# Set places for the softmax exponentials and the first unit rows, squares shared between two engines, and earlier scores of the third batch

## The chip, the core and the metric

One core of a Trainium2 chip runs the whole program. The metric is the device time of one execution in microseconds, so smaller is better; the median of several runs is what kernels are compared by. The engines are TensorE (PE in the profile, its weight loads PEld), VectorE (DVE), ScalarE (ACT), GpSimd (POOL) and SyncE (SP). The last two issue most of the DMA transfers here. Each engine works through its own list of instructions in order, and an instruction whose operands are not ready holds up all that stand behind it in that list.

## What is computed

A channel attention over q, k and v for four batches, and a feed-forward block on its output:

```python
B, N, C = (4, 6080, 256)            # d_ff = 2048
qn = q / (np.linalg.norm(q, axis=1, keepdims=True) + 1e-06)
kn = k / (np.linalg.norm(k, axis=1, keepdims=True) + 1e-06)
s = kn.transpose(0, 2, 1) @ qn / tau
s = s - s.max(-1, keepdims=True)
a = np.exp(s)
a /= a.sum(-1, keepdims=True) + 1e-09
x = (v @ a).reshape(B * N, C)
h = x @ w_in
out = np.maximum(0.01 * h, h) @ w_out
```

The scores s are only 256x256 for each batch, but they sum over all 6080 rows. Since a is small, the kernel multiplies it into w_in once for each batch (w), and the feed-forward block then reads v directly.

## The kernel before

**The feed-forward block.** A batch's 6080 tokens are cut into six tiles of up to 512, 24 tiles in all. A tile is worked off in eight *periods* (d_ff in eight pairs of 128), 192 in all, each about 10 to 12 us long; a period's number is tile times eight plus pair. Each period forms its block of h from seven products of blocks (a Strassen-like scheme; L1197, into the PSUM banks x and z, three passes each over the high and low parts of weights and v) and multiplies the activated blocks by w_out (L1628, into the banks o). ScalarE copies h out of PSUM (L1254), applies the activation (g, L1211) and makes its high part (g_split, L1211 and L1218); VectorE adds to h from PSUM (L1248) and makes the low part (L1222). There is one bank x and one bank z: the next product into them has to wait until ScalarE has read the last one. At a period's end ScalarE copies bank x into bank z (L1243), the *seed copy*, on which the next period's product into z is built up. The last cast of g in a period belongs to the block called C21. From period 48 the feed-forward block works in 16-bit floats, before that in 32-bit ones.

**The attention between it.** While a batch's tiles are worked off, the attention of the next one is woven in by a planner. Steps are put into queues (act, act_late, dve, dve_idle, pe, pe_next) with an estimated length; at fixed places of each period a slot with some room takes the steps that fit, in order, if a step's condition (ready) holds. The number spots[0] counts the visits of TensorE's own queue, three a period. All this happens when the program is written: what stands in the program is a fixed list for each engine.

A batch's scores take 48 chunks of 128 rows, two to a group. For the second and third batch each chunk is cast (L375, ScalarE), its low part is taken (L379, VectorE), its square is added up (L313, L316) and TensorE multiplies it (L408); SCORES_AT gives the period in which this begins. Then follow the norms, the scaled scores (L615), the row maxima nm (L624, VectorE), two exponentials (L630, ScalarE), the turned blocks (L668 and L697 on ScalarE, L676 and L704 on VectorE), and the new weights, whose high and low parts (w_first, w_rest; L866, L878) are stored to DRAM on SyncE's queue (L901) or GpSimd's (L921) and loaded again period by period.

The fourth batch (UNIT) does it another way: ahead of its scores all of q and k is loaded once (L294, GpSimd's queue, three buffers in the tile spare), squared in place by ScalarE (square_ahead, L322) and added up by an accumulating DMA (L327, L325; GpSimd's queue), whose end frees the buffer for the load three groups on. Later the rows are loaded a second time, scaled to unit length (L360, VectorE), cast (unit_high, L366, ScalarE), split (L370, VectorE) and multiplied (L408). The casts write halves of the tile qk_split, of which three exist; the same three hold w_first and w_rest until their stores have read them. The class Splits keeps account of which halves are open.

```python
SCORES_AT = {1: (8, 12), 2: (40, 16), 3: (0, 0)}
...
at(now[0] + 1, put, "act_late", 0.6, lambda j=j: sc.square_ahead(j), then)
...
], ready=splits.free)
```

Of the kernel before, what the change touches and what calls it, by code (L numbers as in the profile page):

```python
# [14 lines left out]
AF = mybir.ActivationFunctionType  # L15
ALU = mybir.AluOpType
AX = mybir.AxisListType

P = 128
QUAD = 32  # L20
TW = 512
G = 2
# [10 lines left out]
TOP = 12  # L33
SUMS_AT = (73, 77, 80, 105)
UNITS = 5
SCORES_AT = {1: (8, 12), 2: (40, 16), 3: (0, 0)}
AHEAD_AT = 49
G_SCALE = 2.0**-19
G_LESS = 2.0**-2
# [4 lines left out]
def channel_attention_ffn(  # L44
# [17 lines left out]
    nc = tc.nc  # L62
    B, N, C = q.shape
    CH = C // P
# [5 lines left out]
    REST = N - RPP * P  # L70
    NCHUNK = RPP + (1 if REST else 0)
# [11 lines left out]
    LEAN = 2  # L83
# [11 lines left out]
    def bank(tag, bufs=1):  # L95
        return psum.tile([P, TW], F32, name="ps_" + tag, tag=tag, bufs=bufs)

    def temp(dtype=F32, name="temp"):
        return work.tile([P, TW], dtype, name=name, tag="temp", bufs=TEMPS)
# [28 lines left out]
    def spare_part(n0, n1):  # L128
        if spare[0] is None:
            spare[0] = const.tile([P, NF * C], F32, name="spare", tag="spare")  # L130
        return spare[0][:, n0 * TW:n1 * TW]
# [26 lines left out]
    class Scale:  # L158
# [3 lines left out]
        def __init__(self, name, parts, bufs=1, near=False):  # L162
            t = small.tile([P, 16], F32, name=name, bufs=bufs)
            self.most = t[:, 0:parts]
            self.top, self.e, self.up, self.down, self.out, self.minus = (t[:, x:x + 1] for x in range(8, 14))
            self.near = near
            if not near:
                self.line = dram.tile([P, 1], F32, name=name + "_line", bufs=bufs)
            self.seen = 0
# [56 lines left out]
    class Splits:  # L226


        def __init__(self):
            self.open, self.half = [], None  # L230

        def free(self, whole=False):
            return self.half is not None and not whole or sum(1 for n in self.open[-3:] if n) < 3 and not (
# [20 lines left out]

        def close(self, n):
            self.open[n] -= 1

    splits = Splits()

# [3 lines left out]
    class Scores:  # L263
# [51 lines left out]
        def add_square(self, sq):  # L315
            return nc.vector.tensor_tensor(out=self.acc[0], in0=self.acc[0], in1=sq, op=ALU.add)  # L316

        def square_ahead(self, j):

            n = REST if REST and j == NCHUNK - 1 else P  # L320
            own = self.chunk(j)[0:n]
            ins = nc.scalar.activation(out=own, in_=own, func=AF.Square)  # L322
            i, x = self.of[j]
            if REST and i == len(self.groups) - 1:
                nc.gpsimd.dma_start(out=self.totals[0:n, :, x, :], in_=own, accum_op=ALU.add)  # L325
            elif x == G - 1:
                nc.gpsimd.dma_start(  # L327
                    out=self.totals.rearrange("p x g c -> p (x g c)"),
                    in_=self.raw[i].rearrange("p x g c -> p (x g c)"), accum_op=ALU.add if i else ALU.bypass,
                )  # L330
            return ins

        def totals_added(self):
            self.total = self.totals[:, :, 0, :]
# [286 lines left out]

        def maxima(self):
            self.nm = small.tile([P, CH], F32, name="nm")
            return nc.vector.tensor_reduce(out=self.nm, in_=self.e, axis=AX.X, op=ALU.max, negate=True)  # L624

        def exps(self):
# [212 lines left out]
    now, w_done, w_stores = [0], {}, []  # L839
# [824 lines left out]
    def at(w, fn, *args):  # L1664
        steps.setdefault(w, []).append((fn, args))

    spots = [0]
# [31 lines left out]
    def put(queue, length, fn, then=(), first=False, ready=lambda: True):  # L1699


        def run():
            ins = fn()
            for entry in then:
                if entry[0] == "call":
                    entry[1](*entry[2:])
                else:
                    put(*entry)
            return ins

        run.ready = ready
        (todo[queue].appendleft if first else todo[queue].append)((length, run))
# [64 lines left out]
    def ahead_work(sc, i):  # L1777

        if i == 0:
            sc.totals = spare_part(6, 8).rearrange("p (x g c) -> p x g c", x=2, g=G)  # L1780
        raw = spare_part(i % 3 * 2, i % 3 * 2 + 2).rearrange("p (x g c) -> p x g c", x=2, g=G)
        sc.load(i, raw, (nc.gpsimd, nc.gpsimd))
        for j in sc.groups[i]:
            then = []
            if j == NCHUNK - 1:
                then = [("call", lambda: at(now[0] + 2, unit_norms, sc))]
            elif j == sc.groups[i][-1] and i + 3 < len(sc.groups):
                then = [("call", ahead_work, sc, i + 3)]
            at(now[0] + 1, put, "act_late", 0.6, lambda j=j: sc.square_ahead(j), then)

    def unit_norms(sc):
        put_steps([
# [6 lines left out]
    def load_next(sc):  # L1799
        if sc.loaded < len(sc.groups):  # L1800
            issued["load"] = sc.load(sc.loaded, qk_raw())
            sc.loaded += 1
# [5 lines left out]
    def unit_go(sc):  # L1808
        while unit_waits and len(unit_ahead) < UNITS and len(unit_temps) < 3:
            unit_one(sc, unit_waits.popleft())  # L1810

    def unit_one(sc, j):
        unit_ahead.append(j)
        unit_temps.append(j)
        t = []

        def unit():
            t.append(temp(name="unit").rearrange("p (x c) -> p x c", x=2))
            ins = sc.unit(j, t[0])
            if j % G == G - 1:  # L1820
                load_next(sc)
            return ins

        def product():
            unit_ahead.pop(0)
            unit_go(sc)
            splits.close(sc.at[j])
            if j == 0:
                sc.begin(None, bank("s"))
            mm = sc.product(j)  # L1830
            if j == NCHUNK - 1:
                norm_work(sc)
            return mm

        def low():
            unit_temps.remove(j)
            unit_go(sc)
            return sc.unit_low(j, t[0])

        def high():  # L1840
            put("act", 0.6, lambda: sc.unit_high(j, t[0]), [
                ("dve", 0.7, low, [("call", lambda: put(
                    "pe_next", 1, product, ready=lambda: (sc.b - 1, "products") in w_done
                ))])
            ], ready=splits.free)

        put("dve", 0.7, unit, [("call", high)])

    def norm_work(sc):
# [18 lines left out]
                ("dve", 0.7, sc.inverse, lambda: not reading[0])]  # L1868

    def softmax(sc):  # L1870
        return [*[("act", 0.65, sc.exps)] * CH,
                ("dve", 1.1, sc.normed), ("call", turn_work, sc)]

    def turn_work(sc):
# [385 lines left out]
    for b in range(1, B):  # L2260
        w0 = (b - 1) * WPB
        sc = scores[b]
        begin, span = SCORES_AT[b]
        when = {j: begin + j * span // NCHUNK for j in range(NCHUNK)}
# [30 lines left out]
    sc, nxt = scores[0], scores[1]  # L2295
# [185 lines left out]
    for i in range(NTILES):  # L2481
        for p in range(NPAIR):
# [15 lines left out]
            x, y, z = bank("x"), bank("z" if i else "y"), None if seeded else bank("z")  # L2498
# [121 lines left out]
```

## Time and profile before

| | us |
|---|---|
| median of three runs | 2030.99 |
| lowest and highest run | 2030.10, 2033.97 |
| the profiled execution | 2031.82 |
| its span, first to last instruction | 2030.04 |
| TensorE busy | 2019.1 |
| VectorE busy | 1684.6 |
| ScalarE busy | 1573.9 |
| GpSimd busy | 394.7 |

The span is the profile's, the median that of the timed runs; the rows further down come from the profiled execution. Times in a timeline count from the span's start. A bracket behind a row gives the time for which that engine was idle before it and the instruction that ended the idle time; a row without one started behind its predecessor.

### The profile page before, as it was taken

The page shows a single profiled execution, that of the slowest core. Times are in us where ns is not written, and L with a number is a line of the kernel's source. Part 1 is how long each engine was busy: PE and PEld are TensorE (multiplying, and loading weights), DVE is VectorE, ACT ScalarE, POOL GpSimd, SP SyncE. Part 2 cuts the span into 40 slices and gives each one's busy share as a digit, 9 for nine tenths or more (in the row PEclk, how much of TensorE's full clock was granted, in tenths as well). Part 3 has the DMA queues.
Part 4 walks back from the last instruction along what each step waited for, and adds up shares of the span by engine and source line. Part 5 has one row for each costly group of instructions (what it writes and reads, how often), then busy time and mean ns, then how long its engine had stood idle before and what let it go on. Part 6 is the DMA issues. An engine that isn't in the chain of part 4 may idle for free.

```text
span 2030.0 us, 28026 instructions
## 1 busy us (share of the span) xinstructions
PE 2019.1 (99%) x9474; PEld 1178.7 (58%) x9474; DVE 1684.6 (83%) x3153; ACT 1573.9 (78%) x2914; POOL 394.7 (19%) x495
## 2 busy tenths in 40 slices
PE   9999999999999999999999999999999999999999
PEld 8888888888885554444555444444444444444444
DVE  7988897787777788779888688989889988988976
ACT  6567886665778888777776678988988888898886
POOL 0000000001002222301000013434333433433342
PEclk9999999999999999999999999999999999999999
DMA  9946784667556977733232325767778876777774
GB/s 361 409 159 225 248 276 150 216 228 202 183 161 223 268 194 201 171 110 108 95 109 93 105 87 120 151 141 145 145 143 192 167 154 135 151 146 145 137 136 95
DMA packets 155727, 349.52 MB, mean 172 GB/s; under 512 B 17824, under 2 KB 49056, under 8 KB 155584
## 3 DMA queue, kind: packets, MB, share of 16 engines
q0 software_dynamic: 62752, 129.07, 32.1%
q1 hardware_dynamic: 92608, 218.48, 31.5%
q8 instruction: 74, 1.21, 0.3%
q14 instruction: 69, 0.57, 0.1%
q10 hardware_dynamic: 224, 0.20, 0.0%
HBM read 188.61 MB, written 57.42 MB: 121 GB/s over the span
## 4 chain that ended last, share of the span: by engine, by line
PE 96%; DVE 2%; ACT 1%; issue 0%; DMA 0%; DVEq 0%; ACTq 0%
PE ps_o L1628 25%; PE ps_x L1197 24%; PE ps_z L1197 18%; PE ps_o L1354 13%; PE ps_s L408 4%; PE ps_y L1354 3%; PE ps_s L1354 3%; PE ps_o L408 2%; PE ps_s L1995 1%; PE ps_y L408 1%; PE ps_y L1995 0%; DVE g_split L1222 0%; DVE h L1248 0%; PE ps_y L825 0%; PE ps_o L1377 0%; PE ps_y L1197 0%
## 5 line engine op out<-in xcount | busy, mean ns | idle before, releaser
L1197 PE MATMUL ps_x<-v_split,w_split 128*128 128x512 f16 (+3 forms) x2280 | 619.6, 380 | 2.6 <-ACT h L1254 2.5
L1628 PE MATMUL ps_o<-g_split,w_out_split 128*128 128x512 f16 (+3 forms) x2496 | 616.1, 382 | 0.0
L1197 PEld LDWEIGHTS <-w_split 128*128 128x128 f16 x3024 | 292.6, 98 | 347.7 <-issue 11.4
L1197 PE MATMUL ps_z<-v_split,w_split 128*128 128x512 f16 (+3 forms) x1704 | 462.1, 380 | 3.1 <-ACT g L1211 2.4
L1248 DVE TENSOR_TENSOR h<-ps_z,h 128x512 f32<-128x512 f32 (+1 forms) x387 | 264.6, 684 | 214.8 <-ACT h L1254 183.2
L1254 ACT COPY h<-ps_x 128x512 f32<-128x512 f32 (+1 forms) x395 | 229.2, 580 | 107.8 <-PE ps_x L1197 96.7
L1222 DVE TENSOR_TENSOR g_split<-g,g_split 128x512 f16<-128x512 f32 (+3 forms) x416 | 281.2, 679 | 9.4 <-ACT g_split L1211 9.1
L1628 PEld LDWEIGHTS ps_o<-g_split,w_out_split 128*128 128x128 f32 x1152 | 216.3, 188 | 44.0
L1628 PEld LDWEIGHTS <-w_out_split 128*128 128x128 f16 x1344 | 131.5, 98 | 156.1
L1313 DVE TENSOR_TENSOR g_pair<-g_b,g_pair 128x512 f16<-128x512 f32 (+1 forms) x262 | 170.9, 680 | 51.8 <-ACT g_pair L1308 51.4
L1354 PE MATMUL ps_o<-g_pair,w_out_split 128*128 128x512 f16 (+1 forms) x774 | 212.8, 377 | 0.4 <-ACT g_pair L1308 0.3
L1211 ACT ACTIVATE g<-h 128x512 f32<-128x512 f32 (+1 forms) x218 | 136.8, 627 | 66.7 <-DVE h L1248 66.7
L1354 PEld LDWEIGHTS <-spare 128*128 128x128 f16 x1032 | 100.9, 98 | 119.7 <-issue 0.7
L1308 ACT CAST g_pair<-g_b 128x512 f16<-128x512 f32 (+1 forms) x262 | 151.1, 611 | 0.0
L1211 ACT ACTIVATE g_split<-h 128x512 f16<-128x512 f32 (+3 forms) x216 | 132.6, 614 | 0.0
L1354 PEld LDWEIGHTS <-w_out_split 128*128 128x128 f16 x774 | 75.7, 98 | 89.9 <-issue 0.6
L1218 ACT CAST g_split<-g 128x512 f16<-128x512 f32 (+3 forms) x200 | 123.4, 617 | 3.3
L1313 DVE TENSOR_TENSOR g_pair<-g_a,g_pair 128x512 f16<-128x512 f32 (+1 forms) x176 | 119.2, 678 | 1.8 <-ACT g_pair L1308 1.1
L1197 PEld LDWEIGHTS ps_x<-v_split,w_split 128*128 128x128 f32 x576 | 107.5, 188 | 21.9 <-ACT g L1211 0.4
L1320 POOL DMA_DIRECT2D g_a<-g_a x86 | 76.6, 891 | 213.7 <-DVE g_pair L1313 179.6
L1320 POOL DMA_DIRECT2D g_a<-g_b x86 | 72.8, 846 | 194.1 <-DMA g_a<-g_a 189.0
L1308 ACT CAST g_pair<-g_a 128x512 f16<-128x512 f32 (+1 forms) x176 | 107.8, 613 | 2.8
(280 smaller groups left out, 2960.8 us busy)
## 6 DMA issues: line engine op xcount, KB each, us to landing
w_split<-w_dram SPq DMA_DIRECT2D x40, 896.0 KB, 6.5
qk_raw<-in_q_dram SPq DMA_DIRECT2D x115, 256.0 KB, 4.5
qk_raw<-in_k_dram SPq DMA_DIRECT2D x115, 256.0 KB, 5.9
v_raw<-in_vT_dram SPq DMA_DIRECT2D x32, 512.0 KB, 4.2
out_dram<-o_sb SPq DMA_DIRECT2D x64, 256.0 KB, 2.9
w_split<-w_dram SPq DMA_DIRECT2D x32, 448.0 KB, 4.1
g_a<-g_a POOLq DMA_DIRECT2D x56, 256.0 KB, 3.2
g_a<-g_b POOLq DMA_DIRECT2D x56, 256.0 KB, 3.2
```

The costliest lines, as they stand in the source:

```text
L408: mm = nc.tensor.matmul(out=out, lhsT=lhsT, rhs=rhs, start=start, stop=stop, skip_group_check=True)
L1197: mm = nc.tensor.matmul(out=ps[:, 0:n], lhsT=w[:, x, a, :], rhs=sp[:, y, 0:n], start=first and k == 0, stop=k == 2, skip_group_check=True,)
L1211: return nc.scalar.activation(out=to, in_=h[:, 0:n], func=AF.Prelu, alpha=0.01, scale=G_SCALE if i >= T16 else 1.0)
L1218: run("act", lambda: nc.scalar.copy(out=sp[:, 0, 0:n], in_=out[:, 0:n]))
L1222: return nc.vector.tensor_tensor(out=sp[:, 1, 0:n], in0=out[:, 0:n], in1=f32(sp[:, 0, 0:n]), op=ALU.subtract)
L1248: issued["dve"] = nc.vector.tensor_tensor(out=h[:, 0:n], in0=ps[:, 0:n], in1=h[:, 0:n], op=ALU.add)
L1254: issued["act"] = nc.scalar.copy(out=h[:, 0:n], in_=ps[:, 0:n])
L1308: return nc.scalar.copy(out=sp[:, 0, 0:n], in_=g32[i, p, HELD.get(name, name)][:, 0:n])
L1313: return nc.vector.tensor_tensor(out=sp[:, 1, 0:n], in0=g32[i, p, HELD.get(name, name)][:, 0:n], in1=sp[:, 0, 0:n], op=ALU.subtract)
L1320: return nc.gpsimd.dma_start(out=g32[i, p, to][:, 0:n], in_=g32[i, p, of][:, 0:n], accum_op=ALU.add)
L1354: issued["pe"] = nc.tensor.matmul(out=ps[:, 0:n], lhsT=fast_lhsT(i, p, prod, x), rhs=sp[:, y, 0:n], start=p == 0 and k == 0, stop=ends and ...
L1628: issued["pe"] = nc.tensor.matmul(out=o_ps[i][j][h][:, 0:n], lhsT=wo_lhsT(i, x, f, h), rhs=sp[:, y, 0:n], start=p == 0 and early and k == ...
```

## The change

Four things are changed. The first exponential of the third batch (LEAN) is put into ScalarE's list only once spots[0] has gone one visit past the one at which the row maxima were issued. The casts of the first six chunks of unit rows wait for *calm*: half of a buffer is open, or the third-last buffer was closed at least two visits ago. The squares of a group of the fourth batch's chunks become available five visits of TensorE's queue after the group's load was written, instead of in the next period, and from the third group on the second chunk of each group is squared on VectorE (product_ahead, queue dve_idle); the accumulating DMA is issued (add_ahead) when both squares of a group are written. And the third batch's scores begin in period 38 instead of 40. In the changed kernel all lines from 230 on have moved down, by 4 at first and by 12 or 13 from line 340 on: L630 is L643, L366 is L378, L1254 is L1267.

```diff
@@ -33,7 +33,7 @@
 TOP = 12
 SUMS_AT = (73, 77, 80, 105)
 UNITS = 5
-SCORES_AT = {1: (8, 12), 2: (40, 16), 3: (0, 0)}
+SCORES_AT = {1: (8, 12), 2: (38, 16), 3: (0, 0)}
 AHEAD_AT = 49
 G_SCALE = 2.0**-19
 G_LESS = 2.0**-2
@@ -227,7 +227,7 @@
 
 
         def __init__(self):
-            self.open, self.half = [], None
+            self.open, self.half, self.shut = [], None, {}
 
         def free(self, whole=False):
             return self.half is not None and not whole or sum(1 for n in self.open[-3:] if n) < 3 and not (
@@ -254,6 +254,10 @@
 
         def close(self, n):
             self.open[n] -= 1
+            self.shut[n] = spots[0]
+
+        def calm(self):
+            return self.free() and (self.half is not None or spots[0] >= self.shut.get(len(self.open) - 3, 0) + 2)
 
     splits = Splits()
 
@@ -315,20 +319,28 @@
         def add_square(self, sq):
             return nc.vector.tensor_tensor(out=self.acc[0], in0=self.acc[0], in1=sq, op=ALU.add)
 
+        def own_rows(self, j):
+            return self.chunk(j)[0:REST if REST and j == NCHUNK - 1 else P]
+
         def square_ahead(self, j):
-
-            n = REST if REST and j == NCHUNK - 1 else P
-            own = self.chunk(j)[0:n]
-            ins = nc.scalar.activation(out=own, in_=own, func=AF.Square)
-            i, x = self.of[j]
+            own = self.own_rows(j)
+            return nc.scalar.activation(out=own, in_=own, func=AF.Square)
+
+        def product_ahead(self, j):
+            own = self.own_rows(j)
+            return nc.vector.tensor_tensor(out=own, in0=own, in1=own, op=ALU.mult)
+
+        def add_ahead(self, i):
             if REST and i == len(self.groups) - 1:
-                nc.gpsimd.dma_start(out=self.totals[0:n, :, x, :], in_=own, accum_op=ALU.add)
-            elif x == G - 1:
+                for x, j in enumerate(self.groups[i]):
+                    own = self.own_rows(j)
+                    n = own.shape[0]
+                    nc.gpsimd.dma_start(out=self.totals[0:n, :, x, :], in_=own, accum_op=ALU.add)
+            else:
                 nc.gpsimd.dma_start(
                     out=self.totals.rearrange("p x g c -> p (x g c)"),
                     in_=self.raw[i].rearrange("p x g c -> p (x g c)"), accum_op=ALU.add if i else ALU.bypass,
                 )
-            return ins
 
         def totals_added(self):
             self.total = self.totals[:, :, 0, :]
@@ -621,6 +633,7 @@
 
         def maxima(self):
             self.nm = small.tile([P, CH], F32, name="nm")
+            self.most_spot = spots[0]
             return nc.vector.tensor_reduce(out=self.nm, in_=self.e, axis=AX.X, op=ALU.max, negate=True)
 
         def exps(self):
@@ -1780,13 +1793,24 @@
             sc.totals = spare_part(6, 8).rearrange("p (x g c) -> p x g c", x=2, g=G)
         raw = spare_part(i % 3 * 2, i % 3 * 2 + 2).rearrange("p (x g c) -> p x g c", x=2, g=G)
         sc.load(i, raw, (nc.gpsimd, nc.gpsimd))
-        for j in sc.groups[i]:
-            then = []
-            if j == NCHUNK - 1:
-                then = [("call", lambda: at(now[0] + 2, unit_norms, sc))]
-            elif j == sc.groups[i][-1] and i + 3 < len(sc.groups):
-                then = [("call", ahead_work, sc, i + 3)]
-            at(now[0] + 1, put, "act_late", 0.6, lambda j=j: sc.square_ahead(j), then)
+        left = [len(sc.groups[i])]
+
+        def done():
+            left[0] -= 1
+            if left[0]:
+                return
+            sc.add_ahead(i)
+            if i + 3 < len(sc.groups):
+                ahead_work(sc, i + 3)
+            elif i == len(sc.groups) - 1:
+                at(now[0] + 2, unit_norms, sc)
+
+        spot = spots[0] + 5
+        for x, j in enumerate(sc.groups[i]):
+            if x and i >= 2:
+                put("dve_idle", 1.0, lambda j=j: sc.product_ahead(j), [("call", done)], ready=lambda: spots[0] >= spot)
+            else:
+                put("act_late", 0.6, lambda j=j: sc.square_ahead(j), [("call", done)], ready=lambda: spots[0] >= spot)
 
     def unit_norms(sc):
         put_steps([
@@ -1842,7 +1866,7 @@
                 ("dve", 0.7, low, [("call", lambda: put(
                     "pe_next", 1, product, ready=lambda: (sc.b - 1, "products") in w_done
                 ))])
-            ], ready=splits.free)
+            ], ready=lambda: splits.calm() if j < 6 else splits.free())
 
         put("dve", 0.7, unit, [("call", high)])
 
@@ -1868,7 +1892,7 @@
                 ("dve", 0.7, sc.inverse, lambda: not reading[0])]
 
     def softmax(sc):
-        return [*[("act", 0.65, sc.exps)] * CH,
+        return [("act", 0.65, sc.exps, lambda: spots[0] >= sc.most_spot + 1 * (sc.b == LEAN)), *[("act", 0.65, sc.exps)] * (CH - 1),
                 ("dve", 1.1, sc.normed), ("call", turn_work, sc)]
 
     def turn_work(sc):
```

The matmuls are the same in number and shape. VectorE has 22 more operations of the form of a square, ScalarE 22 fewer.

ScalarE around the exponentials of the third batch (s_sb, nm). Before, in the middle of a period, between two copies of h:

```order
L1211 ACTIVATE g_7757<-ps_z_7726 128x512
L1254 COPY h_7760<-ps_x_7725 128x512
L1218 CAST g_split_7758<-g_7757 128x512
L630 ACTIVATE s_sb_7763,den_7768<-s_sb_7763,nm_7766 128x256 x2
L1254 COPY h_7782<-ps_x_7725 128x512
L1646 ACTIVATE o_sb_7797<-ps_o_6973,v_scale_6041 128x512
L1211 ACTIVATE g_7803<-h_7782 128x512
L1211 ACTIVATE g_split_7804<-h_7782 128x512
```

Now, at the end of period 63, two squares of the fourth batch's chunks (spare) being near:

```order
L1267 COPY h_7701<-ps_x_7650 128x512
L1224 ACTIVATE g_7718<-h_7701 128x512
L1224 ACTIVATE g_split_7719<-h_7701 128x512
L1224 ACTIVATE g_7730<-ps_x_7650 128x512
L1231 CAST g_split_7731<-g_7730 128x512
L643 ACTIVATE s_sb_7687,den_7734<-s_sb_7687,nm_7705 128x256 x2
L327 ACTIVATE spare_6051<-spare_6051 128x2x256
L1256 COPY ps_z_7752<-ps_x_7751 128x512
```

The two exponentials have moved from ahead of the second h copy to behind the period's last cast; a square and the seed copy (into ps_z) follow.

ScalarE around the first casts of unit rows (into qk_split). Before, from the seed copy on, in period 78:

```order
L1243 COPY ps_z_9220<-ps_x_9219 128x512
L1211 ACTIVATE g_9226<-h_9145 128x512
L1211 ACTIVATE g_split_9227<-h_9145 128x512
L366 CAST qk_split_9230<-unit_9150 128x2x256
L1211 ACTIVATE g_9251<-ps_z_9220 128x512
L1254 COPY h_9254<-ps_x_9219 128x512
L1218 CAST g_split_9252<-g_9251 128x512
L366 CAST qk_split_9230<-unit_9172 128x2x256
L366 CAST qk_split_9263<-unit_9177 128x2x256
L1254 COPY h_9276<-ps_x_9219 128x512
```

Now, from the second h copy of period 78 to the seed copy behind it:

```order
L1267 COPY h_9271<-ps_x_9219 128x512
L1224 ACTIVATE g_9288<-h_9271 128x512
L1224 ACTIVATE g_split_9289<-h_9271 128x512
L1224 ACTIVATE g_9300<-ps_x_9219 128x512
L1231 CAST g_split_9301<-g_9300 128x512
L378 CAST qk_split_9304<-unit_9150 128x2x256
L378 CAST qk_split_9304<-unit_9172 128x2x256
L378 CAST qk_split_9307<-unit_9177 128x2x256
L1256 COPY ps_z_9318<-ps_x_9317 128x512
```

The first cast stood ahead of the g that reads ps_z, and the next two ahead of the h copy; now all three stand behind the period's last cast and ahead of the seed copy of the next period.

ScalarE around the turned block of the third batch (w_a, aT). Before, from its copy out of PSUM to the seed copy:

```order
L668 COPY w_a_7889<-ps_s_7861 128x512
L697 ACTIVATE aT_7892<-w_a_7889 128x128
L697 ACTIVATE aT_7892<-w_a_7889 128x256
L1254 COPY h_7906<-ps_x_7836 128x512
L1211 ACTIVATE g_7923<-h_7906 128x512
L1211 ACTIVATE g_split_7924<-h_7906 128x512
L1211 ACTIVATE g_7935<-ps_x_7836 128x512
L1218 CAST g_split_7936<-g_7935 128x512
L697 ACTIVATE aT_7892<-w_s_7890 128x512
L322 ACTIVATE spare_6001<-spare_6001 128x2x256
L1243 COPY ps_z_7954<-ps_x_7953 128x512
```

Now, from the last cast of period 64 to the seed copy and a few rows behind it:

```order
L1231 CAST g_split_7835<-g_7834 128x512
L681 COPY w_a_7838<-ps_s_7797 128x512
L1659 ACTIVATE o_sb_7856<-ps_o_7025,v_scale_6091 128x512
L710 ACTIVATE aT_7841<-w_a_7838 128x128
L710 ACTIVATE aT_7841<-w_a_7838 128x256
L1256 COPY ps_z_7864<-ps_x_7863 128x512
L1224 ACTIVATE g_7869<-h_7786 128x512
L1224 ACTIVATE g_split_7870<-h_7786 128x512
L710 ACTIVATE aT_7841<-w_s_7839 128x512
```

The copy of the block and its first two high parts stood ahead of an h copy in the middle of a period; now they stand, with an output copy (o_sb), between the last cast and the seed copy.

## Rows read from the trace of the kernel before

**Rows 1.** The page: busy time of the engines, and the chain that ended last.
```profile
PE 2019.1 (99%) x9474; PEld 1178.7 (58%) x9474; DVE 1684.6 (83%) x3153; ACT 1573.9 (78%) x2914; POOL 394.7 (19%) x495
PE 96%; DVE 2%; ACT 1%; issue 0%; DMA 0%; DVEq 0%; ACTq 0%
```

**Rows 2.** Waits of PE: engine, line, waited for, us, times, longest us.
```profile
PE ps_x L1197 <- ACT h L1254: 2.5, 2, 2.1
PE ps_z L1197 <- ACT g L1211: 2.4, 2, 2.1
```

**Rows 3.** Timeline of PE: start us, us, engine, line, operation, count.
```profile
793.12 1.67 PE L1628 MATMUL ps_o<-g_split,w_out_split 128*128 128x512 f16 x7
796.91 0.81 PE L1197 MATMUL ps_x<-v_split,w_split 128*128 128x512 f16 x3 [2.12 <-ACT h L1254]
...
942.47 0.81 PE L1197 MATMUL ps_z<-v_split,w_split 128*128 128x512 f16 x3 [2.05 <-ACT g L1211]
```

**Rows 4.** Timeline of DVE and ACT around the first of these waits.
```profile
794.58 0.69 DVE L624 TENSOR_REDUCE nm<-s_sb 128x2 f32<-128x512 f32 x1
795.30 0.51 ACT L630 ACTIVATE s_sb<-s_sb,nm 128x256 f32<-128x256 f32 x1 [2.79 <-DVE nm L624]
...
796.30 0.56 ACT L1254 COPY h<-ps_x 128x512 f32<-128x512 f32 x1
```

**Rows 5.** Timeline of POOL and ACT around the second.
```profile
937.59 1.38 POOL L921 DMA_DIRECT2D w_dram<-w_first  x2 [9.29 <-DVE w_first L878]
...
941.30 0.62 ACT L366 CAST qk_split<-unit 128x512 f16<-128x512 f32 x1 [2.88 <-DMA w_dram<-w_first]
```

**Rows 6.** Pieces of the chain that ended last: start us, us, what, count.
```profile
863.10 0.65 PE ps_x L1197 x3
...
872.81 0.65 PE ps_x L1197 x3
...
937.59 3.61 DMA w_dram<-w_first
```

**Rows 7.** Lines L322 and L316: count, duration ns min/median/max.
```profile
L322 ACT ACTIVATE spare<-spare x48: 612/617/627, 635.5 to 856.1; 128x512 f32<-128x512 f32 x47, 64x512 f32<-64x512 f32 x1
...
L316 DVE TENSOR_TENSOR sq_acc<-sq_acc,sq x32: 650/685/687, 600.2 to 757.3; 128x512 f32<-128x512 f32 x32
```

**Rows 8.** A window: busy PE, PEld, DVE, ACT, POOL; PEclk, DMA share, GB/s.
```profile
680.00:730.00 50.00, 50.00 (x241) 26.29 (x240) 36.15 (x61) 43.94 (x83) 12.71 (x19) 1.00 0.97 288
```

**Rows 9.** Timeline of ACT and PE in period 65.
```profile
804.97 0.60 ACT L668 COPY w_a<-ps_s 128x512 f32<-128x512 f32 x1
...
809.64 0.62 ACT L697 ACTIVATE aT<-w_s 128x512 f16<-128x512 f32 x1
...
810.69 0.58 ACT L1243 COPY ps_z<-ps_x 128x512 f32<-128x512 f32 x1
...
811.67 0.81 PE L1197 MATMUL ps_z<-v_split,w_split 128*128 128x512 f16 x3
```

**Rows 10.** Timeline of ACT and PE at the first unit rows' scores.
```profile
947.35 0.62 ACT L1218 CAST g_split<-g 128x512 f16<-128x512 f32 x1
...
949.80 2.13 PE L408 MATMUL ps_s<-qk_split 128*128 128x256 f16 x18
```

**Rows 11.** Timeline of SP near 496 us, and line L901: issue to landing.
```profile
496.19 0.52 SPq L901 DMA_DIRECT2D w_dram<-w_first  x1
...
DMA to landing us min/median/max: 5.9/5.9/5.9
```

**Rows 12.** Timeline of DVE and POOL; line L327: durations, issue to landing.
```profile
785.42 0.68 DVE L1222 TENSOR_TENSOR g_split<-g,g_split 128x512 f16<-128x512 f32 x1
785.54 0.95 POOL L327 DMA_DIRECT2D spare<-spare  x1
...
L327 POOL DMA_DIRECT2D spare<-spare x23: 557/942/1270, 645.2 to 853.1; - x23
...
DMA to landing us min/median/max: 4.5/6.1/10.7
```

## Prediction

> **What bounds the kernel now.** I first read the busy shares and the chain of work that ended last [rows 1]: TensorE is busy for 99% of the span and is 96% of the chain, so only time in which TensorE stands still can be won; VectorE's 83% and ScalarE's 78% count only where they make it wait. The list of TensorE's waits [rows 2] then names what there is: two waits for the copy of h (L1254), 2.5 us in all, the longest 2.1, and two for the activation g (L1211), 2.4 us, the longest 2.1. The granted clock is 1.00 in the stretch [rows 8], the upper of its two levels, 2.4 GHz; nothing is to be had there.
>
> The timeline places the two long waits. Three matmuls take 0.65 us from start to start [rows 6], one 0.216. Seven that began at 793.12 should hand over at 794.63; the next starts at 796.91: **2.28 us lost** [rows 3]. The row itself says 2.12, because it counts from the modelled end; the second wait, 2.05 at 942.47, is by the same difference **2.21 us lost**. Together 4.49 us: that is the whole prize in the stretch that the change rewrites (about 499 to 960 us).
>
> *The first.* ScalarE had the two softmax exponentials of the third batch at the head of its list and stood 2.79 us for the row maxima nm, which VectorE only began at 794.58. The copy of h that TensorE needs stood behind both exponentials and began at 796.30 [rows 4]. *The second.* The first cast of unit rows (L366) needs a buffer whose last content, w_first, was still being stored: the stores were issued at 937.59, and the chain counts 3.61 us to their landing [rows 5, 6]. ScalarE stood 2.88 us, and the g that TensorE needs stood behind the cast.
>
> **The change part by part.**
>
> *Exponentials.* They now wait for the next visit of TensorE's list after the maxima are issued. By the order they stand at the end of period 63, behind the last cast of the period, and no longer ahead of an h copy. Between the add of h that precedes the maxima and the first exponential ScalarE has four operations (g, high part, g, cast), 4 x 0.53 = 2.1 us (0.53 from start to start, two from 809.64 to 810.69 [rows 9]); VectorE has one subtraction and the maxima, 0.68 + 0.69 = 1.4 us [rows 4, 12]. So nm should be there 0.7 us early, and 2.28 us go. What is late next: the copy that seeds the next product (L1243). In period 65 two extra operations, 1.05 us, stand ahead of it, it begins at 810.69, takes 0.58, and the product that reads it starts at 811.67 without a wait, 0.40 us after it ended [rows 9]. Now two exponentials (795.30 to 796.30, 1.00 us [rows 4]) and a square (0.53) stand there: 0.48 us more. **+0.1 us.**
>
> *First unit rows.* The cast waits until half a buffer is open or the third-last buffer was closed two visits ago. It moves from in front of g to the end of the period, with two more casts behind it. The last cast of that period stands at 947.35 [rows 10]; with the 2.2 us gone it is at 945.1, and the unit casts follow at 945.7, 4.5 us after the stores had landed (937.59 + 3.61 = 941.20): no wait, and 2.21 us go. What is late next: three casts, 1.6 us, stand ahead of the seed copy, 0.54 us more than in period 65; but now 12 matmuls of the scores, which took 2.13 us for 18 [rows 10], 1.4 us for 12, come between the copy and its reader. The scores in turn need the casts and VectorE's low parts; by the order I count those ready half a microsecond ahead. **0.**
>
> *VectorE squares part of the chunks.* 22 of 48 squares leave ScalarE (22 x 0.617 = 13.6 us) and come to VectorE, where an f32 operation of 128x512 takes 0.685 us (22 x 0.685 = 15.1 us) [rows 7]. In the fullest stretch ScalarE is busy 43.9 and VectorE 36.2 of 50 us [rows 8], so 15 us over some 200 fit; no square is on TensorE's path. **0**, unless one holds up an add of h: the last rival.
>
> *Scores of the third batch two periods earlier.* TensorE's matmuls are the same in number and shape. Two things ride on it. First, the casts of period 38 now follow soon on the weights of the second batch and need buffers that SyncE's stores (L901) must have read. The one that decides was issued at 496.19 and lands 5.9 us later [rows 11], at 502.1; its cast stands at about 501.5 by the order. 0.6 us late is about what the slack of a seed copy takes up (0.40 us [rows 9]), and the copies there have nothing else in front: 0 us; bounds 0 and, if the store takes 2 to 3 us longer, 2.1. Second, what follows the scores is repacked. At the end of period 64 an eviction (0.60 us, L668), an output copy and two high parts (0.53 each, as above) stand ahead of the seed copy, 1.66 us and so 0.61 more than in period 65: 0.2 us beyond the slack. In the same place VectorE has the low parts and differences of the turned block in one piece ahead of an add of h. Bounds 0 (the reader comes later) and 0.7 us (both late together); **+0.2 us**, by the nearest row, the copy at 810.69.
>
> **Sum.** -2.28 - 2.21 + 0.1 + 0.2 = -4.2 us. On the profiled execution, 2031.82 us with a span of 2030.0, that is 2027.6. That execution is 0.83 us above the median of the runs; on the median, 2030.99, it is **2026.8 us**. A measurement of this kernel can tell about 0.2%, 4.06 us, from no change; the forecast of 0.21% lies just beyond it.
>
> **A rule that speaks against it.** At 785.42 VectorE began a subtraction of two SBUF operands, 0.68 us; at 785.54 GpSimd issued an accumulate in 0.95 us, against a median of 0.94 [rows 12]. The Trainium skill, page "SBUF — State Buffer", section "SBUF: two separate sides", has VectorE and GpSimd share a pair of ports under an exclusive lock, which a VectorE operation with two SBUF inputs can hold against a GpSimd operation that reads SBUF. By that rule each of the 22 squares could push back an issue of GpSimd's by up to 0.68 us, and I would double the chance of the last rival. The row shows no such push, so the sum and the chance go without it.
>
> **The rivals.**
>
> *One stall comes back, 2028.9 us.* The waits are for the same resources, only the places move. If the store before period 38 takes 2 to 3 us longer than 5.9 (an accumulate's longest landing is 1.75 times its median [rows 12]), or if VectorE, now with squares in its list, ends the maxima 1 us later than I count, ScalarE stands with an h copy behind it: 2.1 us, as before. For it: margins of 0.5 to 0.7 us, read from an order. Against: ScalarE and VectorE are idle 6 to 14 of 50 us.
>
> *Many small latenesses, 2028.0 us.* Both engines now work in fuller clusters ahead of seed copies, whose slack is 0.4 us. Four or five places with 0.2 to 0.3 us each, 1.2 us: 2028.0, within 0.2%. For it: the end of period 63 and of 64 both come out just beyond the slack.
>
> *Slower: squares that wait for their loads, 2036 us.* A group's load is issued behind the accumulate that frees its buffer, and its squares stand five visits later in the lists, whether the data is there or not. Five visits are 5/3 of a period of 9.71 us (863.10 to 872.81 [rows 6]), 16.2 us. Accumulate and load follow one another on GpSimd's queue; with the load bounded by the accumulate's landing, 6.1 us at the median and 10.7 at the longest [rows 12], they take 12.2 and at worst 21.4 us, 5.2 too late. Then an add of h stands on VectorE behind the square: 4.8 us of TensorE after the slack. Break-even with the kernel before is at 4.2 us, one such group; slower by 0.2% needs 8.3, two groups: 2026.8 + 9.6 = 2036.4. For it: in the fullest stretch the DMA share is 0.97 [rows 8]. Against it: no square of the kernel before held anything up that TensorE's waits show [rows 2], and the medians leave 4 us.
>
> **How the numbers follow.** Both stalls gone and at most 0.4 us in their place, 2026.4 to 2026.9: 0.50, faster. Many small latenesses: 0.29, within 0.2%. One stall back: 0.16, within 0.2% as well. Slower: 0.05, of which 0.04 by over 0.2%. So faster 0.50, same 0.46, slower 0.04. The range reaches down to all 4.49 us gone and the lowest of the runs before (2030.1 - 4.49 = 2025.6, taken as 2025.7) and up just past one stall back (2029.2).
>
> **What would show it.** TensorE's waits for h and g should keep under 0.5 us in all between 499 and 960 us; ScalarE's waits for nm and for the stores of w_first should be gone or under 0.3 us. There should be 26 squares on ScalarE and 22 on VectorE at 0.68 us. Near the end of period 64 (about 810 us) TensorE should wait 0.2 us for the seed copy. I am wrong if TensorE's lost time falls by less than 3 us, if ScalarE waits for a store near 500 us, or if VectorE's squares show waits for their loads.

## The result and the profile after

The changed kernel takes 2044.54 us at the median (2042.15 to 2045.42, six runs), the one before 2031.83 in six runs; the ratio is 1.0059, with a 95% interval of 1.0046 to 1.0072. It is **slower by 0.6%**, 12 us, where 0.2% less was forecast; the range ended at 2029.2. The profiled execution has a span of 2042.9 us, 12.8 more than before (2042.86 against 2030.04).

The waits of TensorE after (engine, line, waited for, us in all, times, longest), against [rows 2]:

```profile
PE ps_z L1210 <- ACT g L1224: 10.0, 3, 6.2
PE ps_z L1210 <- ACT ps_z L1256: 2.0, 1, 2.0
PE ps_x L1210 <- ACT h L1267: 1.4, 2, 1.0
PE ps_z L1210 <- DVE h L1261: 0.8, 2, 0.6
```

The two waits that were to go are gone: the exponentials and the first unit rows hold up nobody. In their place are three longer ones, 3.53, 2.02 and 6.21 us, all between 696 and 734 us. The list of ScalarE's and VectorE's waits names their source, the squares:

```profile
ACT spare L327 <- DMA spare<-in_k_dram: 12.7, 4, 6.0
ACT qk_split L387 <- DMA w_dram<-w_first: 1.9, 1, 1.9
DVE spare L331 <- DMA spare<-in_k_dram: 4.9, 2, 2.8
```

The longest, in the timeline of POOL, ACT and PE (start, us, engine, line, operation, idle before):

```profile
728.33 0.54 POOL L298 DMA_DIRECT2D spare<-in_k_dram  x1
...
732.41 0.63 ACT L327 ACTIVATE spare<-spare 128x512 f32<-128x512 f32 x1 [6.04 <-DMA spare<-in_k_dram]
732.95 0.58 ACT L1224 ACTIVATE g<-ps_z 128x512 f32<-128x512 f32 x1
...
733.58 1.44 PE L1210 MATMUL ps_z<-v_split,w_split 128*128 128x512 f16 x3 [6.21 <-ACT g L1224]
```

The square of a chunk stands at the head of ScalarE's list, its load has only been issued at 728.33, and the g that TensorE needs stands behind it. Why the load was so late is in the chain that ended last (pieces: start, us, what), which now runs through the transfers:

```profile
692.05 10.75 DMA spare<-spare
...
703.61 0.53 POOL spare L298
704.14 4.02 DMA win_whole<-win_sums
...
709.25 7.58 DMA spare<-spare
...
718.22 9.29 DMA spare<-spare
...
728.33 4.06 DMA spare<-in_k_dram
```

Each accumulate (spare<-spare) takes 7.6 to 10.8 us here, the loads wait for it on GpSimd's queue, and the next accumulate stands right behind the load. Once the row stops for something else: from 704.14 on GpSimd waits 4.0 us for a transfer of other work (new weights, win_whole), and the accumulate of 709.25, whose squares had ended at 697.1, stands behind it. So the row has a pace of its own, made of accumulates and loads and of what else is on GpSimd's queue.

A second loss had no term in my sum. Around the waits of 3.53 and 6.21 us TensorE's clock fell to its lower level, 1.2 of 2.4 GHz. Windows (busy PE, PEld, DVE, ACT, POOL; PEclk; DMA share; GB/s):

```profile
700.00:705.00 5.00, 4.59 (x15) 2.52 (x15) 0.13 (x1) 2.98 (x6) 1.62 (x3) 0.66 0.59 154
700.64:704.06 3.42, 3.42 (x11) 1.94 (x10) 0.00 (x0) 1.75 (x4) 0.98 (x2) 0.50 0.47 145
731.36:738.19 6.83, 4.62 (x12) 2.35 (x12) 0.00 (x0) 3.71 (x7) 2.19 (x4) 0.50 1.04 206
```

In the last two stretches the granted clock is 0.50, where it was 1.00 before [rows 8], and TensorE works for 3.42 and 4.62 us in them. Half of that time would have done: 0.5 x 3.42 + 0.5 x 4.62 = 4.0 us lost. The balance: three waits 11.8, the clock 4.0, one new wait near 503 us 1.0, one for an h add 0.6, less the two old waits 4.2, makes 13.2 us. Counted in order, both kernels have 9474 matmuls. From the one that starts at 480 us in the kernel before to the one that starts there at 1000 us it takes 520.02 us, and the changed kernel 533.26: 13.2 us more. The spans differ by 0.4 us less, for reasons ahead of 480 us and behind 1000, where nothing was changed.

### The profile page after: what moved, and what is told of

Read it like the earlier page. It is cut to its first block, busy times and chain, and to the rows that moved or that the text cites. A ratio compares the mean times of both kernels' runs of the same rounds, so it can differ in the third digit from the quotient of the medians.

```text
span 2042.9 us, 28068 instructions
## 1 busy us (share of the span) xinstructions
PE 2021.3 (99%) x9474; PEld 1179.0 (58%) x9474; DVE 1697.6 (83%) x3175; ACT 1564.6 (77%) x2892; POOL 393.7 (19%) x495
## 4 chain that ended last, share of the span: by engine, by line
PE 92%; DMA 3%; DVE 2%; ACT 1%; issue 1%; POOL 0%; SPq 0%; POOLq 0%; ACTq 0%; DVEq 0%
PE ps_o L1641 24%; PE ps_x L1210 23%; PE ps_z L1210 17%; PE ps_o L1367 13%; PE ps_s L420 4%; PE ps_y L1367 3%; PE ps_s L1367 3%; DMA spare<-spare 2%; PE ps_o L420 2%; PE ps_s L2019 1%; PE ps_y L420 1%; DVE h L1261 0%; DVE g_split L1235 0%; PE ps_y L838 0%; PE ps_o L1390 0%
## 5 line engine op out<-in xcount | busy, mean ns | idle before, releaser
L1267 ACT COPY h<-ps_x 128x512 f32<-128x512 f32 (+1 forms) x395 | 229.7, 581 | 116.8 <-PE ps_x L1210 105.6
```

The lines of the kernel that those rows point to most:

```text
L1267: issued["act"] = nc.scalar.copy(out=h[:, 0:n], in_=ps[:, 0:n])
```

## The experiments

Each kernel is told from the changed one or the one before by its edit. Theory A says that the squares run through the lists faster than loads and accumulates can follow; B, that the earlier scores crowd the transfers; C, that VectorE's squares hold GpSimd off; D, that two engines on one group are the harm whatever the pace.

**The third part undone** (e1), all else as changed:

```diff
-        spot = spots[0] + 5
         for x, j in enumerate(sc.groups[i]):
-            if x and i >= 2:
-                put("dve_idle", 1.0, lambda j=j: sc.product_ahead(j), [("call", done)], ready=lambda: spots[0] >= spot)
-            else:
-                put("act_late", 0.6, lambda j=j: sc.square_ahead(j), [("call", done)], ready=lambda: spots[0] >= spot)
+            at(now[0] + 1, put, "act_late", 0.6, lambda j=j: sc.square_ahead(j), [("call", done)])
```

> The changed kernel with its third part undone: all 48 squares of the fourth batch's chunks on ScalarE again, each put into its queue in the period after its group's load; the exponentials, the unit-row casts and the scores from period 38 stay changed. Theory A (the squares overtake the chain of loads and accumulates on GpSimd's queue): the three long waits of TensorE between 695 and 734 us (3.5, 2.0 and 6.2 us) are gone, the two stalls of the kernel before are gone too, about 1.2 us stay near 503 us: 2027 to 2029 us. Theory B (the scores that begin two periods earlier bring loads into the stretch that make the chunks' loads late): the waits between 695 and 734 us stay, 2038 us or more. Theory C (VectorE's squares hold GpSimd off): as A, 2027 to 2029 us.

2028.62 us, ratio 0.9976 (0.9967 to 0.9986), span 2026.6. TensorE's waits:

```profile
PE ps_x L1210 <- ACT h L1267: 0.4, 1, 0.4
PE ps_z L1210 <- ACT ps_z L1256: 0.4, 1, 0.4
PE ps_z L1210 <- ACT g L1224: 0.3, 1, 0.3
```

Of these only the seed copy's 0.4 us, at 800 us, lies in the stretch that was changed; the other two (1247.6 and 275.1 us) stand in the kernel before as well. So B falls: without the third part both stalls are gone and no long wait comes in their place. This version beats both kernels.

**The third part alone**, in the kernel before (e2: the other three parts undone).

> The kernel before with the third part of the change alone: squares five visits after the load's place in the program, 22 of them on VectorE; the rest as before. Theory A: squares wait for their loads between 680 and 740 us, TensorE loses 8 to 15 us there, and the two stalls of the kernel before may stay: 2038 to 2048 us. Theory B: no such waits, 2031 us within 2. Theory C: as A.

2042.25 us in one run. ScalarE's squares wait 5.5 us for loads, VectorE's 5.7, and TensorE waits 5.24 us for g at 697.57 and 1.89 at 724.78; the wait behind the exponentials is still there (ScalarE 3.2 us for nm). The harm comes with the third part by itself.

**No accumulates after the first group** (e4; the sums of squares are left incomplete):

```diff
-            else:
+            elif i == 0:
                 nc.gpsimd.dma_start(
                     out=self.totals.rearrange("p x g c -> p (x g c)"),
```

> The changed kernel without the accumulating transfers after the first group: the sums of squares of the fourth batch are left incomplete, 22 transfers of 512 KB are gone, and a group's load waits for the squares alone. Theory A: the loads are issued 7 to 11 us earlier, no square waits for its load, TensorE's three waits of 3.5, 2.0 and 6.2 us are gone: 2028 to 2031 us. Theory C: the loads' issues stay slow beside VectorE's squares and some waits of 2 us or more remain between 690 and 740 us.

2027.67 us in one run. No square waits for a load; the largest waits of TensorE under the lines concerned are

```profile
PE ps_z L1210 <- DVE h L1261: 0.7, 2, 0.5
PE ps_x L1210 <- ACT h L1267: 0.4, 1, 0.4
```

The only one of them in the changed stretch is one of 0.5 us, at 776.1. With 22 squares on VectorE at the same places of the lists, taking the accumulates out of the row of transfers takes all of the loss away. That speaks for A and against C and D. It also takes 22 transfers of 512 KB off the DMA engines, so by itself it does not tell the row on GpSimd's queue from the load on these engines; e9, further down, leaves the transfers in.

**VectorE's squares with the old timing** (e3): both kinds of squares put into their queues in the period after the load, `at(now[0] + 1, put, ...)`, with the five visits taken out.

> The changed kernel, with 22 squares on VectorE as in the change, but each square put into its queue in the period after its group's load, as in the kernel before, and not five visits after it. This tells the engine from the timing. Theory A: if two engines still finish a group's squares sooner than the accumulates land, waits stay but shrink; if the pace falls back to about 11 us for a group, they go: 2027 to 2036 us. Theory C (the squares on VectorE slow GpSimd's issues and so the loads): waits stay as long as in the changed kernel, 2040 us or more, and GpSimd's issues of accumulates take longer than 1.0 us at the median.

2073.45 us, a miss for both theories' numbers: far worse than the change. TensorE and ScalarE:

```profile
PE ps_z L1210 <- ACT g L1224: 33.6, 9, 11.4
ACT spare L327 <- DMA spare<-in_k_dram: 37.7, 9, 6.8
```

So the sharing does not need the five visits to do harm; they hold it down. (Five visits with all squares on ScalarE were not run.) What drives it is when, and how fast, the lists ask for the squares once two engines do them. The places can be read from the traces, by ScalarE's seed copies, of which one opens each period: 55.18 is about a fifth of the way through period 55. The place of the first square of the sixth and of the tenth group, and the periods for each of the four groups between, beside the waits of squares for loads on ScalarE and VectorE:

```
kernel               6th     10th    periods a group   waits, us
before               55.18   59.18   1.00              0
e1, part 3 undone    55.18   59.21   1.01              0
e9, paced            54.95   58.95   1.00              2.2 + 3.2, later groups
e5, six visits       54.95   58.39   0.86              8.3 + 6.5
e3, next period      53.95   56.93   0.75              37.7 + 12.7
changed              54.95   57.44   0.62              12.7 + 4.9
e6, four visits      54.95   57.42   0.62              10.8 + 7.6
e2, part 3 alone     54.95   57.33   0.60              5.5 + 5.7
```

In the kernels that keep a period for each group no square of these groups waits for its load; in those that fall below it squares wait. The column of waits is not in the order of the pace, since the start counts too: e3 stands a whole period ahead of the others.

The chain's own pace is read from the loads' issues on GpSimd in the changed kernel: 681.96, 690.98, 703.08, 717.12, 727.80 for the sixth to the tenth group, 11.5 us each, with the stop of 4.0 us for win_whole in it; in e1, where no square waits, 11.9 (679.6 to 727.1). The paced kernel e9 has such a stop as well (4.49 us before 709.39) and no square waits there, so the stop alone is not the cause. A period is 11.3 us in this stretch of the kernel before (its squares of the second to the eleventh group end their periods at 655.9 and 757.7). In the change the lists ask for the tenth group 2.49 periods, about 28.1 us, after the sixth; the loads landed 44.2 us apart (688.18 and 732.39). The sixth group's square, at 692.47, had 4.3 us to spare. That leaves 11.8 us as an estimate; ScalarE's three waits for these loads come to 12.3 and the three waits of TensorE to 11.8.

**Six visits for the first ten groups** (e5), `spot = spots[0] + (6 if i < 10 else 5)`:

> The changed kernel with the squares of the first ten groups six visits of TensorE's list after the load's place, not five; the later groups at five; 22 squares on VectorE as in the change. Theory A (pace of the squares against the pace of the chain of loads and accumulates): a round of three groups takes about 3.3 us longer in the lists, so the lateness that has grown by the tenth group falls by up to 10 us: the three waits of TensorE between 690 and 735 us are gone or under 1 us each, 2027 to 2031 us. Theory C (VectorE's squares hold GpSimd off): the number of squares on VectorE is the same, so waits of several us remain: 2036 us or more.

2036.33 us, ratio 1.002 (1.0011 to 1.003): measured from e1, half of the loss, not all of it, a miss for the size. Up to the ninth group the first squares now stand a period apart; the tenth stands 0.44 of a period behind the ninth, and there ScalarE's waits begin (4.0 us). The two longest of TensorE, 3.36 and 2.88 us, end at 734.05 and 758.66.

**Four visits** (e6), `spots[0] + 4`:

> The changed kernel with all squares four visits after the load's place, not five. Theory A: the squares run further ahead of the chain, TensorE waits more often and longer than in the changed kernel: over 2050 us. Theory C: the squares on VectorE are as many, so about the same as the changed kernel, 2040 to 2048 us.

2043.5 us in one run: as the changed kernel, which by its text spoke for C. The lists explain it: up to the eleventh group the squares stand at the same places as with five visits, so the visits do not bind there. What binds instead, the slots' room perhaps, was not looked into. The kernel does not tell A from C.

**The sharing kept, the pace set** (e9):

```diff
+    paced = [0]
...
-        spot = spots[0] + 5
+        spot = max(spots[0] + 5, paced[0] + 3 if 3 <= i <= 12 else 0)
+        paced[0] = spot
```

> The changed kernel with the sharing kept (22 squares on VectorE), and one rule more: the squares of the groups 3 to 12 become available no sooner than three visits (one period) after those of the group before. By the order the second squares of these groups then stand a period apart, as in the kernel before, where in the change five groups take 3.5 periods. Theory A (pace against the chain of loads and accumulates, some 11 us for a group): the waits between 690 and 735 us go or stay under 1 us each, and what is left are later groups without the rule: 2027 to 2031 us. Theory D (two engines squaring for one group, or VectorE's squares themselves, whatever the pace): waits of 2 us or more remain there, 2035 us or more.

2029.35 us, ratio 0.9983 (0.9974 to 0.9992). Between 690 and 735 us TensorE has no wait any more, and its clock stays at 1.00:

```profile
700.00:705.00 5.00, 5.00 (x27) 2.52 (x25) 4.60 (x8) 4.60 (x9) 1.63 (x3) 1.00 0.90 260
730.00:735.00 5.00, 5.00 (x27) 2.93 (x25) 2.84 (x6) 3.29 (x7) 0.00 (x0) 1.00 0.84 232
```

Later groups, without the rule, still wait, 3.2 us once on VectorE and 2.2 in two places on ScalarE, of which TensorE sees 1.1 at most. As the cause of the loss C and D fall: VectorE squares as many chunks, and the three long waits are gone. Sharing is not free even so: between the same matmuls as above e9 takes 519.13 us, 2.0 more than e1 (517.15). GpSimd's issues of accumulates tell the same of C. Before their median was 0.94 us [rows 12]; in the changed kernel (count, ns min/median/max):

```profile
L340 POOL DMA_DIRECT2D spare<-spare x23: 557/925/1197, 651.2 to 855.0; - x23
```

**The other parts.** The earlier scores alone (e7), the calm casts alone (e8), and exponentials and calm casts without the rest (e10), each set into the kernel before:

> The kernel before with the fourth part alone: the third batch's scores begin in period 38. In the order this by itself puts the exponentials behind the period's last cast. Expected by my own sum: the wait of 2.12 us for the h copy behind the exponentials is gone, the one of 2.05 us for g behind the first unit-row cast stays, and a wait of 0.4 to 1.2 us stands near 503 us: span 2028.5 us. If the exponentials' own rule were what removes the first wait, it would stay: span 2030.5 us.

> The kernel before with the second part alone: the first casts of unit rows wait until a half is open or the third-last buffer was closed two visits ago. Expected: the wait of 2.05 us for g at about 942 us is gone, that of 2.12 us behind the exponentials at about 797 us stays, nothing new: span 2027.8 us. A rival, that the three casts ahead of the seed copy make it late: a wait of 0.3 to 0.6 us near 948 us in its place.

> The kernel before with the first and second parts alone: exponentials one visit after the maxima, calm unit-row casts; squares and the start of the scores as before. By the order both land behind the period's last cast, as in the changed kernel. Expected from the two single parts measured: both waits of about 2.1 us gone, no wait near 503 us, no late copies near 800 us beyond 0.3 us: 4.2 to 4.5 us under the kernel before, ratio 0.9978. If the earlier scores were needed to free the place of the exponentials, a wait of 1 to 2 us for a seed copy or an h copy stays near 797 us: ratio 0.9985.

The longest waits of TensorE under the lines concerned, in e7, then e8, then e10:

```profile
PE ps_z L1210 <- ACT g L1224: 2.7, 2, 2.4
PE ps_x L1210 <- ACT h L1267: 0.7, 2, 0.4
```

```profile
PE ps_x L1210 <- ACT h L1267: 2.5, 2, 2.1
PE ps_z L1210 <- ACT g L1224: 0.3, 1, 0.3
```

```profile
PE ps_z L1210 <- DVE h L1261: 1.6, 2, 1.4
PE ps_z L1210 <- ACT ps_z L1256: 0.7, 1, 0.7
```

By the waits, e7 and e8 came out nearly as written: the earlier scores take the first wait away and leave the second (2.41 us here), the calm casts the other way round; the wait near 503 us that e7 was to show is not there. Their spans, 2030.2 and 2029.0, are 1.7 and 1.2 us above what was expected, in single runs, and the traces say why. In e8 the old wait of 2.11 us, which was left in, was followed by the lower clock:

```profile
796.47 0.81 PE L1210 MATMUL ps_x<-v_split,w_split 128*128 128x512 f16 x3 [2.11 <-ACT h L1267]
...
797.58:801.00 3.42, 3.42 (x9) 1.22 (x8) 3.35 (x10) 2.95 (x6) 0.71 (x1) 0.50 0.70 223
```

(the second row is a window). That is 0.5 x 3.42 = 1.7 us which the kernel before did not lose after its wait of 2.12. e7 was 0.7 us behind before 480 us, where nothing was changed: TensorE waited 0.9 us for a first load there. Most of the rest comes from eight small latenesses between 782 and 857 us, 1.8 us in all, of which the next section tells. e10 is 2029.74 us, ratio 0.9987 (0.9977 to 0.9996), the second branch of its text: without the earlier scores, the exponentials at their set place cost a wait for an h add (1.4 us) and one for the seed copy (0.7).

What each part is worth is told by the time between the same matmuls as above, 520.02 us in the kernel before. The calm casts win 2.2 us (e8, its 1.7 us of clock left out), the earlier scores 0.5 (e7), calm casts and exponentials 2.3 together (e10), and all three 2.9 (e1). So the second stall's 2.2 us are won in full, and of the first stall's 2.28 most is lost again in its place, with the earlier scores or without them.

## Why the prediction was wrong, point by point

- *What bounds the kernel, and the prize of 4.49 us*: right as far as the waits go; both are gone in the changed kernel and in e1. The prize leaves out the clock, which sometimes falls after such a wait (e8).
- *Exponentials, +0.1, and first unit rows, 0*: right; no wait for nm or for w_first's store near 942 us is left, and no seed copy behind them costs more than 0.4 us.
- *Earlier scores, +0.2*: too small. e1 shows 0.4 us of waiting for a seed copy, and by the starts of its matmuls eight places between 781 and 856 us, this one among them, where a product into z starts 0.1 to 0.5 us late, 1.8 us in all. Most are too short for the list of waits; e7 has the same eight, the kernel before none. That is the rival "many small latenesses", with more places than its four or five. Near 503 us the store took longer than the 5.9 us that I took [rows 11]: issued at 495.25, and its cast began at 502.75 after 1.85 us of waiting. In the changed kernel that is 1.0 us of TensorE; in e1, where ScalarE waited 0.8, no wait of TensorE is listed there.

```profile
495.25 0.52 SPq L914 DMA_DIRECT2D w_dram<-w_first  x1
...
502.75 0.62 ACT L387 CAST qk_split<-qk_raw 128x512 fp32r<-128x512 f32 x1 [1.85 <-DMA w_dram<-w_first]
```

- *The sum of these three parts, -4.2 us*: e1 measures a ratio of 0.9976, 4.9 us with 2.8 to 6.7 for its interval. The number agrees, but partly by luck. Between the same matmuls e1's trace is only 2.9 us shorter than that of the kernel before, which happened to keep its clock at 1.00 after both stalls. Of the 13 runs of the kernel before that were timed beside e1, the six with a mean granted clock of 1.000 took 2031.95 to 2032.36 us and the four with 0.998 took 2034.74 to 2035.97, while all ten runs of e1 have 1.000. One fall as in e8, 1.7 us, is 0.0008 of the span, so two of them would make 0.998; those runs were not traced, and this part stays an estimate.
- *VectorE squares part of the chunks, 0*: **the step that failed.** I asked whether 15 us of work fit beside other work, and they do; I did not ask what becomes due sooner when two engines do what one did. Before, ScalarE's slots took one square at a time, a group in a period of 11.3 us, and the transfers need 11.5; in the change the groups came 0.62 of a period apart, and in place of nothing stand three waits of TensorE, 11.8 us, and 4.0 us of lower clock.
- *The rival "squares that wait for their loads"* had the mechanism in part, the place on GpSimd's queue and, for one group, a size of the right order (4.8 us; it was three waits of 2.0 to 6.2, and 2044.5 us where it had 2036.4), but 5 in 100 for a chance. It looked for the harm on VectorE, in front of an add of h; the three long waits came from ScalarE, where g and a seed copy stood behind a square. Its error is the sentence "Five visits are 16.2 us". They count from where the load stands in the lists. On the chip the load waits there for its accumulate, and that stands behind the load and the accumulate before it, so lateness is handed from group to group; I priced each group as if it began on time, against a landing of 6.1 us at the median over the whole stretch, where it is 7.6 to 10.8 in the fullest part. In the changed kernel the squares of the seventh group end at 699.96; their accumulate is issued at 718.22 and the load written behind it at 727.80, 28 us later. The 16.2 us themselves were too short (a period is 11.3 us in this stretch, not 9.71, so 18.8), and that did not help. The trace of before hinted at it, in GpSimd's list of waits:

```profile
POOL spare L294 <- DMA spare<-spare: 94.9, 19, 7.6
```

GpSimd waits for 19 of 23 accumulates before it may load, and [rows 8] has a DMA share of 0.97: a row of transfers with little slack, that nothing should feed faster.
- *The rule on the shared ports*: no run shows such a push; the accumulates' issue times (0.925 us at the median with VectorE's squares, 0.942 without) and e9 speak against a cost here. The rule of the Trainium skill's page "SBUF — State Buffer", section "SBUF: two separate sides", is about a GpSimd operation that reads SBUF; that the issuing of a transfer is one was an assumption of the prediction.
- *The signs of being wrong*: all three came, TensorE's lost time, ScalarE's wait for a store near 500 us and VectorE's squares waiting for loads.

## What to carry to other kernels

An engine that does a step slowly may be the governor of a chain of transfers behind it. Before work is spread over two engines, compare the pace at which the lists will then ask for data with the pace of the chain that delivers it, over several rounds and in its fullest stretch, not one round against a median. If the pace can be written into the order, as in e9, nearly all of the harm goes; but the engine that is relieved was not the bound here, so sharing won nothing either, and e1, without it, has the lowest ratio of the kernels that keep the sums whole.

## What was not expected of the hardware

TensorE's clock fell to its lower level at some waits and not at others, and the length of the wait does not tell which. It fell at those of 3.53 and 6.21 us in the changed kernel (4.0 us lost beyond their length) and at those of 2.11 us in e8 and in e2 (1.7 us lost each). It did not after 2.02 us in the changed kernel, 2.12 and 2.05 in the kernel before [rows 3], 2.41 in e7 and even 3.36 in e5 (734.05 us; PEclk 1.00 in the 5 us behind it). The same stall behind the exponentials went without a fall in one trace and with one in another. A stall can be dearer than its length, and a single trace does not show whether it is.
